# Three small edits to an attention and mixture-of-experts kernel: a padded tile, another order of the first pair's products, earlier gates for attention

## The chip, the cores and the metric

The kernel runs on one core of one Trainium2 chip. The metric is the time on the device in microseconds; the median of three runs of the kernel before is 916.73 us.

## The reference, cut to what matters

Block-causal attention (4 batches, 8 heads, 576 rows, 64 columns a head, blocks of 64 rows), and its output, laid out as 2304 rows of 512, goes through four experts whose outputs are summed with normalised weights. All is float32.

```python
scores = scale * np.matmul(q, k.transpose(0, 1, 3, 2))
scores = np.where(block_i >= block_j, scores, -1000000000.0)
attn = softmax(scores)
x = np.matmul(attn, v) 
p = domain_probs / (domain_probs.sum(-1, keepdims=True) + 1e-09)
for e in range(4):
    h = np.maximum(x @ w1[e], 0.0)      # 512 -> 1024
    out += p[:, e:e + 1] * (h @ w2[e])  # 1024 -> 512
```

## The kernel before, in words

**Precision.** A float32 product is made of three matmuls of type fp32r on split operands: each operand is a high part (a cast) and a low part (operand less high part), and high x high, high x low and low x high are summed in PSUM. Names ending in h and l are these parts (w1h, w1l, xh, xl, hh, hl). The cast is a_copy() (line 344), the subtraction tt() (line 351).

**Blocks.** The 2304 rows are five blocks (BLOCKS): block 0 is the first 64 rows of each batch (256 rows), blocks 1 to 4 the other 512 rows of batch 0 to 3. Blocks 0 to 2 go through the experts in 96 chunks (4 experts x 8 slices of 128 hidden columns, three times): chunk i is mm1(i) (line 1012: 12 matmuls that make 128 hidden columns for all rows of the block), relu(), and mm2 (line 1062: 12 matmuls that add the chunk's part to four accumulators), one chunk behind. Blocks 3 and 4 go together (both_blocks()): mm1 of both blocks for two slices of hidden columns at once is a Winograd form of Strassen's scheme, 7 products in place of 8 (product(), line 1235, 6 matmuls each), for 16 pairs j of slices; mm2_half() (line 1298) does their second layer, 48 matmuls a pair from the third pair on.

**A pair's products.** CHAIN lists the products in the order in which they are issued, each with a role 0, 1 or 2, that is, the PSUM bank that it adds to: (1,0), (2,1), (6,0), (7,2), (5,0), (4,2), (3,0). Products 1 and 2 read the x of block 3 (xh, xl), 6 reads S2, 7 S3, 5 S1, 4 A22 and 3 S4, sums and differences of the two blocks' x. Between two products of a bank a copy of the bank is taken by ScalarE (snap(), line 1255: V1 after product 1, U2 after 6, V7 after 7, U4 after 5), and the next product to that bank waits for it. SHARE says how many groups of second-layer matmuls are issued behind each product; pair 0 has only four such groups (the last chunk's mm2), which go behind products 1 and 2, and pair 1 has none.

**prepare().** When the last attention unit is through and all of attention's buffers are free, the pool attn is closed and the pool pair is laid in its place; it holds A22, S2, S3, S1 and S4 (high and low, 128 x 1024 each), four more buffers each of hh, hl and o, two more of w1h, w1l, w2h and w2l (in the trace these carry a p at the end: hhp, w1hp) and four sc. prepare() then makes, mostly on VectorE: the split of A22, s1, s3, s2, the splits of S2, S3 and S1, s4 and the split of S4, in that order.

**The pools.** The pool const holds what lives through the kernel (weights' buffers, xh, xl, hh, hl, o, XR, ident, probs_n and last probs_s). The pools attn and pair are laid behind it.

**The order of the work.** There are no hand-written queues: Flow.run() is a planner with costs for each engine. It takes one operation after the other from many generator threads by modelled start time and priority, and so fixes the order of instructions on each engine; what waits for what is then by semaphores. Attention is cut in 16 units (one batch, two heads); the first four have no gate (-1), the other twelve may start loading when the planner is at chunk gate[u], which rises in equal steps from GATES[0] to GATES[1]. A unit loads k, q and v, transposes k and q on VectorE (kT, qT), splits them (KK, HH, LL), makes the scores on TensorE (lines 520, 521), the maxima over GpSimd (mx, line 686), the exponentials on ScalarE, the sums (sa on VectorE, sb on GpSimd, line 665) and the product with v (line 732), and scales it (x of the last two blocks: tile xr, line 351).

Of the kernel before, what the change touches and what calls it, by code (L numbers as in the profile page):

```python
# [8 lines left out]
F32 = mybir.dt.float32  # L9
# [11 lines left out]
BLOCKS = [[(b, 0, MASK_BLOCK) for b in range(4)]] + [[(b, MASK_BLOCK, 576)] for b in range(4)]  # L21
# [8 lines left out]


CHAIN = [(1, 0), (2, 1), (6, 0), (7, 2), (5, 0), (4, 2), (3, 0)]
SHARE = [2, 2, 2, 3, 2, 2, 3]

GATES = (28.0, 84.0)

WARM = 9

# [171 lines left out]
def kernel(  # L210
# [14 lines left out]
    P = 128  # L225
# [37 lines left out]
    const = ctx.enter_context(tc.tile_pool(name="const", bufs=1))  # L263
# [19 lines left out]
    XR = [const.tile([P, KC, MAXW], F32, name=f"xr{g}") for g in range(2)]  # L283
    ident = const.tile([P, P], F32, name="ident")
    probs_n = const.tile([P, len(BLOCKS) * 4, E], F32, name="probs_n")
    probs_s = const.tile([P, len(BLOCKS) * 4], F32, name="probs_s")
    const.seal()
    attn = short.enter_context(tc.tile_pool(name="attn", bufs=1))
    for tag, n, shape, dt in (
# [37 lines left out]
    def op(eng, cost, fn, r=(), u=(), prio=0.0):  # L327
        p = prio if callable(prio) else (lambda: prio)
        return Op(eng, cost, fn, r, u, p)
# [18 lines left out]
    def tt(eng, dst, a, b, alu, n, r, u, prio=0.0):  # L348
        both = {"dve": 1.04 * n + 70, "pool": 2.1 * n + 365}
        engs = [(e, both[e]) for e in (eng if isinstance(eng, list) else [eng])]  # L350
        o = op(engs, 0, lambda e: ENG[e].tensor_tensor(out=dst, in0=a, in1=b, op=alu), r, u, prio)  # L351
        o.port = a.space != PSUM and b.space != PSUM
        return o
# [755 lines left out]
    def prepare():  # L1109

        yield ("until", lambda: len(raw_x) == 2 * KC and all(len(fl.free[x]) == n for x, n in counts.items()))
        base = max(b.base for x in counts for b in fl.free[x])
        short.close()
        more = ctx.enter_context(tc.tile_pool(name="pair", bufs=1, reuse_waits="tile"))

        def add(tag, n, shape, dt=F32):
            for k in range(n):
                fl.give(late_buf(more.tile(shape, dt, name=f"{tag}p{k}"), tag, base))

        def late_buf(t, tag, base):  # L1120
            b = Buf(t, tag)
            b.last = base
            return b

        names = ("A22", "S2", "S3", "S1", "S4")
        xt = {x: [late_buf(more.tile([P, 2, MAXW], F32R, name=f"{x}{y}"), None, base) for y in "hl"] for x in names}
        for y in xt.values():
            for b in y:
                b.base = base
        add("hh", 4, [P, MAXW], F32R)  # L1130
        add("hl", 4, [P, MAXW], F32R)
        add("w1h", 2, [P, DM], F32R)
        add("w1l", 2, [P, DM], F32R)
        add("w2h", 2, [P, DM], F32R)
        add("w2l", 2, [P, DM], F32R)
        add("w1r", 1, [P, KC, P])
        add("o", 4, [P, DM])
        fl.add_bufs("sc", [])
        add("sc", 4, [P, MAXW])
        n = 2 * MAXW  # L1140
        x2, x3 = [Buf(x, None) for x in XR]
        a11, a12, a21, a22 = [x[:, k:k + 2, :] for x in XR for k in (0, 2)]
        dv = [raw_x[k] for k in raw_x]

        def split(x, src, deps, u):
            hi, lo = xt[x]
            a = yield a_copy(hi.tile, src, n, deps, [hi, u], 0.5)
            l = yield tt("dve", lo.tile, src, hi.tile, SUB, n, deps + [a], [hi, lo, u], 0.5)
            xp[x] = (hi.tile, lo.tile, [a, l])
            return [a, l]  # L1150

        got = yield from split("A22", a22, dv, x3)
        s1 = yield tt("dve", a22, a21, a22, ADD, n, dv + got, [x3], 0.5)
        s3 = yield tt("dve", a21, a11, a21, SUB, n, dv + [s1], [x2, x3], 0.5)
        yield ("until", lambda: len(xready.get((PAIR, KC - 1), ())) == 2)
        old = [v for c in range(KC) for v in xready[PAIR, c]]
        s2 = yield tt("dve", a11, a22, a11, SUB, n, [s1, s3] + old, [x2, x3], 0.5)
        yield from split("S2", a11, [s2], x2)
        yield from split("S3", a21, [s3], x3)
        yield from split("S1", a22, [s1], x3)  # L1160
        s4 = yield tt("dve", a12, a12, a11, SUB, n, [s2] + old, [x2], 0.5)
        yield from split("S4", a12, [s4], x2)
        for x, r in zip((x2, x3), XR):
            for k in range(KC):
                fl.give(late_buf(r[:, k, :], "sc", x.last))
# [11 lines left out]
    def both_blocks():  # L1177

        n = MAXW
        for x, src in (("xh", "hh"), ("xl", "hl")):  # L1180
            b = yield fl.take(x, PAIR + 1)
            for k in range(KC):
                y = Buf(b.tile[:, k, :], src)
                y.last = b.base
                fl.give(y)
        yield ("until", lambda: PAIR in X and X[PAIR] is not None and "sc" in fl.free)
        xhb, xlb = X[PAIR]
        rest = [(NC - 1, t) for t in range(4)]
        for j in range(len(pairs)):
            now[0] = NC + 2 * j  # L1190
            if j > 1:
                m, t = j // 2 - 1, j % 2
                rest = [(m, t, c, k) for c in range(4) for k in range(4)]
            st, banks = {}, {}
            for (i, role), share in zip(CHAIN, SHARE):
                yield from product(j, i, role, banks, st)
                for _ in range(min(share, len(rest))):
                    x = rest.pop(0)
                    yield from (mm2(*x) if len(x) == 2 else mm2_half(*x))
            while rest:  # L1200
                x = rest.pop(0)
                yield from (mm2(*x) if len(x) == 2 else mm2_half(*x))
        now[0] = NC + 2 * len(pairs)
        for t in range(2):
            for c in range(4):
                for k in range(4):
                    yield from mm2_half(len(pairs) // 2 - 1, t, c, k)

    def product(j, i, role, banks, st):
        n = MAXW  # L1210
        yield ("until", lambda: (j, i) in wp)
        (wh, wl, va, vl), s = wp[j, i]
        if i in (1, 2):
            yield ("until", lambda: all(len(xready.get((PAIR, 2 * (i - 1) + k), ())) == 2 for k in range(2)))
            xhb, xlb = X[PAIR]
            k = slice(2 * i - 2, 2 * i)
            xh, xl, xv = xhb.tile[:, k], xlb.tile[:, k], [v for k in range(2) for v in xready[PAIR, 2 * (i - 1) + k]]
        else:
            name = {3: "S4", 4: "A22", 5: "S1", 6: "S2", 7: "S3"}[i]
            yield ("until", lambda: name in xp)  # L1220
            xh, xl, xv = xp[name]
        start = role not in banks
        if start:
            banks[role] = yield fl.take("h", None, ("att",))
        pb = banks[role]
        before = {6: "V1", 5: "U2", 3: "U4", 4: "V7"}.get(i)
        if before:
            yield ("until", lambda: before in st)
        ps = pb.tile

        def fn(_):
            for kc in range(2):
                ks = slice((2 * s + kc) * P, (2 * s + kc + 1) * P)
                for m, (w, x) in enumerate(((wh, xh), (wh, xl), (wl, xh))):
                    nc.tensor.matmul(out=ps[:, :n], lhsT=w.tile[:, ks], rhs=x[:, kc, :n], start=(start and kc == 0 and m == 0),  # L1235
                                     stop=(i in (2, 3, 4) and kc == 1 and m == 2), skip_group_check=True)

        mm = yield op("pe", 6 * (n / 2.4 + PEO), fn, [va, vl] + xv + ([st[before][1]] if before else []), [pb, wh, wl], 3.0)
        done = i in (2, 7, 4, 3)
        if done:  # L1240
            fl.give(wh, wl)
        if i in (1, 6, 5, 7):
            fl.spawn(snap(st, {1: "V1", 6: "U2", 5: "U4", 7: "V7"}[i], pb, mm))
        if i == 2:
            fl.spawn(total(j, 0, 0, st, pb, mm, "V1"))
        if i == 4:
            fl.spawn(total(j, 1, 0, st, pb, mm, "U2"))
            fl.spawn(total(j, 1, 1, st, None, None, "U4"))
        if i == 3:
            fl.spawn(relu_pair(j, 0, 1, pb, mm, True))  # L1250
# [75 lines left out]
    for ph, jobs in enumerate(PLAN):  # L1326
        for _ in range(sum(len(cs) for _, cs, _ in jobs)):
            gate.append(-1.0 if ph <= 1 else GATES[0] + (GATES[1] - GATES[0]) * (len(gate) - 4) / 11)
    u = ua = us = ju = pu = 0
# [13 lines left out]
    for c in range(KC):  # L1343
        fl.spawn(first_half(c))
    fl.spawn(prepare())
    kz = Val(2000.0, "pool")
    fl.fill = warm_up
# [44 lines left out]
```

## Time and profile before

| what | us |
| --- | --- |
| median of three runs | 916.73 |
| lowest and highest | 916.69, 922.09 |
| the profiled execution | 917.19 |
| its span, first to last instruction | 915.4 |
| TensorE busy | 900.3 |
| VectorE busy | 694.0 |
| ScalarE busy | 451.9 |
| GpSimd busy | 142.3 |

The profiled execution's time is 1.8 us more than its span. PE is TensorE, PEld its weight loads, DVE VectorE, ACT ScalarE, POOL GpSimd. L1298 is line 1298 of the kernel before. A matmul's own duration (389 ns and the like) is longer than the distance to the next one, since they are pipelined.

### The profile page before, as it was taken

Reading aid. Unit: us, or ns where it says so; the run is one execution under the profiler, and the core shown is the slowest. Engines: PE = TensorE matmul, PEld = TensorE weight load, DVE = VectorE, ACT = ScalarE, POOL = GpSimd, SP = SyncE. Lnnn points to the kernel's source line nnn. Section 1 sums busy time; section 2 is a strip of 40 time slices with the busy share of each in tenths; the row PEclk is TensorE's granted clock in tenths of the full one; section 3 lists DMA queues with packets and bytes.
Section 4 is the critical chain, followed back from the end, with each engine's and each line's share of the span. In section 5 each row is a group of like instructions: output and inputs, shape, how many; then the busy total and the mean of one; then the engine's idle time right before and its main releaser. Section 6 shows DMA issues by size and latency. Waiting matters only on the chain.

```text
span 915.4 us, 12377 instructions
## 1 busy us (share of the span) xinstructions
PE 900.3 (98%) x4301; PEld 713.8 (78%) x4302; DVE 694.0 (76%) x1296; ACT 451.9 (49%) x859; POOL 142.3 (16%) x53
## 2 busy tenths in 40 slices
PE   8999999999999999999999999799999999999998
PEld 4677788787777877877787877588888888888886
DVE  6799998797988988997988988965565655666542
ACT  3587766556546556656654543545243333333220
POOL 1101110404124134143242132000000000000000
PEclk9899999999999999999999999999999999999999
DMA  9876557463365355445435323311121212110002
GB/s 182 166 200 176 145 126 219 103 153 83 93 144 120 104 129 113 127 119 120 118 104 119 83 87 95 110 53 58 34 70 34 71 35 69 47 47 24 11 1 93
DMA packets 214655, 91.18 MB, mean 100 GB/s; under 512 B 130368, under 2 KB 195904, under 8 KB 214592
## 3 DMA queue, kind: packets, MB, share of 16 engines
q1 hardware_dynamic: 211424, 89.59, 38.4%
q10 hardware_dynamic: 3168, 0.79, 0.6%
q8 instruction: 34, 0.56, 0.3%
q14 instruction: 29, 0.24, 0.1%
HBM read 85.63 MB, written 4.72 MB: 99 GB/s over the span
## 4 chain that ended last, share of the span: by engine, by line
PE 90%; DVE 5%; SPq 2%; DMA 2%; issue 1%; ACT 0%; POOL 0%; DVEq 0%; POOLq 0%; ACTq 0%
PE h L1012 22%; PE acc L1062 22%; PE acc L1298 19%; PE h L1235 9%; PE att L1235 6%; PE att L732 4%; SPq L338 2%; PE att L520 2%; PE att L521 2%; PE att L508 1%; PE acc L732 1%; DMA S<-in_v_dram 1%; DVE o L1099 1%; PE acc L508 1%; DVE xr L351 1%
## 5 line engine op out<-in xcount | busy, mean ns | idle before, releaser
L1012 PE MATMUL h<-xl,w1h 128*128 128x512 f32 (+1 forms) x384 | 136.8, 356 | 2.1 <-DVE xl L351 2.1
L1012 PE MATMUL h<-xh,w1h 128*128 128x512 f32 (+1 forms) x384 | 137.4, 358 | 0.0
L1012 PE MATMUL h<-xh,w1l 128*128 128x512 f32 (+1 forms) x384 | 136.8, 356 | 0.0
L1062 PE MATMUL acc<-w2h,hh 128*128 128x512 f32 x320 | 126.7, 396 | 0.0
L1062 PE MATMUL acc<-w2l,hh 128*128 128x512 f32 x320 | 125.2, 391 | 0.0
L1062 PE MATMUL acc<-w2h,hl 128*128 128x512 f32 x320 | 125.1, 391 | 0.0
L665 POOL PARTITION_ALL_REDUCE sb<-sa x24 | 82.2, 3474 | 138.1 <-DVE sa L351 121.7
L344 ACT CAST w2h<-w2r 128x512 fp32r<-128x512 f32 x115 | 71.5, 622 | 55.9 <-PE acc L1062 41.7
L686 POOL PARTITION_ALL_REDUCE mx<-cm x16 | 56.0, 3499 | 277.1 <-DVE cm L351 260.6
L351 DVE TENSOR_TENSOR w2l<-w2r,w2h 128x512 fp32r<-128x512 f32 x118 | 83.3, 707 | 11.4 <-ACT w2h L344 11.2
L351 DVE TENSOR_TENSOR w1l<-w1r,w1h 128x512 fp32r<-128x512 f32 (+1 forms) x126 | 84.5, 671 | 3.9 <-ACT w1h L344 2.8
L1012 PEld LDWEIGHTS h<-xl,w1h 128*128 128x128 f32 x384 | 73.0, 190 | 13.2 <-DVE xl L351 2.5
L1012 PEld LDWEIGHTS h<-xh,w1h 128*128 128x128 f32 x384 | 72.9, 190 | 12.2 <-issue 1.2
L1012 PEld LDWEIGHTS h<-xh,w1l 128*128 128x128 f32 x384 | 73.0, 190 | 10.2
L1029 ACT ACTIVATE hh<-h 128x512 fp32r<-128x512 f32 (+1 forms) x96 | 50.5, 526 | 60.1 <-PE h L1012 59.9
L344 ACT CAST w1h<-w1r 128x512 fp32r<-128x512 f32 (+1 forms) x115 | 68.4, 595 | 14.6 <-PE att L1235 5.3
L344 ACT COPY S<-att 128x512 f32<-128x512 f32 (+2 forms) x94 | 50.5, 538 | 45.3 <-DVE att L590 34.7
L1062 PEld LDWEIGHTS acc<-w2h,hh 128*128 128x128 f32 x320 | 60.2, 188 | 12.9 <-issue 1.7
L1062 PEld LDWEIGHTS acc<-w2h,hl 128*128 128x128 f32 x320 | 60.1, 188 | 13.1
L1062 PEld LDWEIGHTS acc<-w2l,hh 128*128 128x128 f32 x320 | 60.3, 188 | 10.4
L1031 DVE SCALAR_TENSOR_TENSOR hl<-h,hh 128x512 fp32r<-128x512 f32 (+1 forms) x96 | 56.8, 592 | 10.6 <-ACT hh L1029 9.9
L351 DVE TENSOR_TENSOR S<-S,mx 128x1024 f32<-128x1024 f32 (+4 forms) x80 | 59.8, 792 | 3.0 <-POOL mx L686 3.0
(323 smaller groups left out, 1815.5 us busy)
## 6 DMA issues: line engine op xcount, KB each, us to landing
w2r<-in_moe_w_dram SPq DMA_DIRECT2D x128, 256.0 KB, 2.9
w1r<-in_moe_w_dram SPq DMA_DIRECT2D x121, 256.0 KB, 2.9
qr<-in_q_dram SPq DMA_DIRECT2D x112, 64.0 KB, 2.7
kr<-in_k_dram SPq DMA_DIRECT2D x64, 72.0 KB, 3.6
VN<-in_v_dram SPq DMA_DIRECT2D x32, 128.0 KB, 2.6
out_dram<-o SPq DMA_DIRECT2D x12, 256.0 KB, 2.1
w1rp<-in_moe_w_dram SPq DMA_DIRECT2D x7, 256.0 KB, 3.0
out_dram<-op SPq DMA_DIRECT2D x4, 256.0 KB, 2.5
```

The source lines that it names most:

```text
L338: o = op(q, 550.0, lambda e: (nc.sync if e == "sp" else nc.scalar).dma_start(out=dst, in_=src), r, u, prio)
L344: o = op(engs, 0, lambda e: nc.scalar.copy(dst, src) if e == "act" else nc.vector.tensor_copy(dst, src), r, u, prio)
L351: o = op(engs, 0, lambda e: ENG[e].tensor_tensor(out=dst, in0=a, in1=b, op=alu), r, u, prio)
L665: sums.append((yield op("pool", 150 + 6.3 * W, lambda _, h=h: nc.gpsimd.partition_all_reduce(sb.tile[:, h * W:h * W + W], sa.tile[:, h * W ...
L686: lambda _: nc.gpsimd.partition_all_reduce(mx.tile[:, :2 * W], src, P, RED.max),
L732: nc.tensor.matmul(out=x.tile[64 * g:64 * g + 64, W - w:W], lhsT=lhsT, rhs=rhs, start=(i == 0), stop=(i == len(todo) - 1))
L1012: nc.tensor.matmul(out=ps[:, :n], lhsT=s.tile[:, ks], rhs=x.tile[:, kc, :n], start=(kc == 0 and m == 0), stop=(kc == KC - 1 and m == 2),)
L1029: a = yield op("act", 0.833 * n + 55, lambda _: nc.scalar.activation(hh.tile[:, :n], ps[:, :n], AF.Relu), [mm], [pb, hh], 0.0)
L1031: l = yield op("dve", 1.04 * n + 70, lambda _: nc.vector.scalar_tensor_tensor(out=hl.tile[:, :n], in0=ps[:, :n], scalar=0.0, in1=hh.tile[: ...
L1062: nc.tensor.matmul(out=acc, lhsT=s.tile[:, ts], rhs=w.tile, start=(f == 0 and m == 0), stop=(f == FC - 1 and m == 2))
L1235: nc.tensor.matmul(out=ps[:, :n], lhsT=w.tile[:, ks], rhs=x[:, kc, :n], start=(start and kc == 0 and m == 0), stop=(i in (2, 3, 4) and kc ...
L1298: nc.tensor.matmul(out=acc, lhsT=s.tile[:, ts], rhs=w.tile, start=(c == 0 and x == 0), stop=(c == 3 and x == 2))
```

## The change

The tile probs_s gets 32 columns in place of 20 (128 bytes a partition in place of 80). Pair 0 issues its products in the order FIRST; which product gives back a pair of weight buffers is changed with it. prepare() splits S3 right after s3 is formed, ahead of s2. The last gate is chunk 82 in place of 84.

```diff
 CHAIN = [(1, 0), (2, 1), (6, 0), (7, 2), (5, 0), (4, 2), (3, 0)]
+FIRST = [(1, 0), (2, 1), (7, 2), (4, 2), (6, 0), (5, 0), (3, 0)]
 SHARE = [2, 2, 2, 3, 2, 2, 3]
-GATES = (28.0, 84.0)
+GATES = (28.0, 82.0)
...
-    probs_s = const.tile([P, len(BLOCKS) * 4], F32, name="probs_s")
+    probs_s = const.tile([P, 32], F32, name="probs_s")
...
         s3 = yield tt("dve", a21, a11, a21, SUB, n, dv + [s1], [x2, x3], 0.5)
+        yield from split("S3", a21, [s3], x3)
         yield ("until", lambda: len(xready.get((PAIR, KC - 1), ())) == 2)
         old = [v for c in range(KC) for v in xready[PAIR, c]]
         s2 = yield tt("dve", a11, a22, a11, SUB, n, [s1, s3] + old, [x2, x3], 0.5)
         yield from split("S2", a11, [s2], x2)
-        yield from split("S3", a21, [s3], x3)
         yield from split("S1", a22, [s1], x3)
...
-            for (i, role), share in zip(CHAIN, SHARE):
+            for (i, role), share in zip(CHAIN if j else FIRST, SHARE):
...
-        done = i in (2, 7, 4, 3)
+        done = i in ((2, 7, 4, 3) if j else (2, 6, 5, 3))
```

## Rows read from the trace of the kernel before

**Rows 1.** The page: busy us (share) xinstructions; chain that ended last by engine.

```profile
PE 900.3 (98%) x4301; PEld 713.8 (78%) x4302; DVE 694.0 (76%) x1296; ACT 451.9 (49%) x859; POOL 142.3 (16%) x53
...
PE 90%; DVE 5%; SPq 2%; DMA 2%; issue 1%; ACT 0%; POOL 0%; DVEq 0%; POOLq 0%; ACTq 0%
```

**Rows 2.** Windows: stretch; PE, PEld, DVE, ACT, POOL busy (x); PEclk; DMA; GB/s.

```profile
330.00:430.00 100.00, 99.92 (x474) 79.27 (x473) 89.41 (x173) 61.11 (x115) 30.80 (x9) 1.00 0.50 124
...
552.00:564.00 12.00, 12.00 (x61) 8.96 (x61) 8.86 (x15) 3.84 (x7) 6.19 (x2) 1.00 0.23 66
564.00:574.00 10.00, 10.00 (x45) 8.07 (x43) 10.00 (x15) 4.33 (x7) 0.00 (x0) 1.00 0.50 157
574.00:590.00 16.00, 11.40 (x45) 7.96 (x44) 15.93 (x25) 8.63 (x15) 0.00 (x0) 1.00 0.25 80
...
589.50:911.50 322.00, 321.88 (x1386) 260.13 (x1386) 183.29 (x317) 112.94 (x195) 0.00 (x0) 1.00 0.16 46
```

**Rows 3.** Timeline of TensorE, pairs 0 to 2: start, us, what [idle before, releaser].

```profile
573.77 0.39 PE L1062 MATMUL acc<-w2h,hl 128*128 128x512 f32 x1
574.56 0.49 PE L1235 MATMUL att<-S2h,w1h 128*128 128x512 f32 x1 [0.40 <-ACT S2h L344]
576.53 0.50 PE L1235 MATMUL att<-S2l,w1h 128*128 128x512 f32 x1 [1.48 <-DVE S2l L351]
576.86 0.40 PE L1235 MATMUL att<-S2h,w1l 128*128 128x512 f32 x1
...
586.78 0.40 PE L1235 MATMUL att<-xh,w1lp 128*128 128x512 f32 x1
589.57 0.47 PE L1235 MATMUL h<-S2h,w1h 128*128 128x512 f32 x1 [2.40 <-DVE w1h L344]
...
596.85 0.39 PE L1235 MATMUL att<-xh,w1hp 128*128 128x512 f32 x1
```

**Rows 4.** The chain that ended last, chunks of blocks 1 and 2: start, us, what.

```profile
299.43 2.72 PE h L1012 x12
302.15 2.72 PE acc L1062 x12
...
463.61 2.81 PE acc L1062 x12
```

**Rows 5.** Groups by form, line 1298: | busy us, mean ns of one | idle.

```profile
L1298 PE MATMUL acc<-w2h,hhp 128*128 128x512 f32 x84 | 33.2, 395 | 0.0
...
L1298 PE MATMUL acc<-w2hp,hh 128*128 128x512 f32 x24 | 9.5, 396 | 0.0
...
L1298 PE MATMUL acc<-w2h,hh 128*128 128x512 f32 x24 | 9.3, 389 | 0.0
...
L1298 PE MATMUL acc<-w2hp,hhp 128*128 128x512 f32 x20 | 7.8, 391 | 0.0
```

**Rows 6.** Timelines of VectorE and ScalarE: the last unit's end, prepare(), pair 1's w1h.

```profile
563.79 0.69 DVE L351 TENSOR_TENSOR xr<-xs,rc 128x512 f32<-128x512 f32 x1
...
569.75 1.22 DVE L351 TENSOR_TENSOR xr<-xr,xr 128x1024 f32<-128x1024 f32 x1
...
589.00 0.43 DVE L344 CAST w1h<-w1r 128x512 fp32r<-128x512 f32 x1
...
564.52 1.05 ACT L344 CAST A22h<-xr 128x1024 fp32r<-128x1024 f32 x1 [0.58 <-DVE xr L351]
```

**Rows 7.** Timelines of TensorE and ScalarE: a snapshot of a bank, and a cast.

```profile
569.69 0.39 PE L1235 MATMUL att<-xh,w1l 128*128 128x512 f32 x1
...
570.17 0.59 ACT L1255 COPY scp<-att 128x512 f32<-128x512 f32 x1 [2.97 <-PE att L1235]
...
573.46 1.05 ACT L344 CAST S2h<-xr 128x1024 fp32r<-128x1024 f32 x1 [2.18 <-DVE xr L351]
```

**Rows 8.** The chain that ended last, VectorE's part before 589 us: start, us, what.

```profile
581.76 1.14 DVE S4l L351
```

**Rows 9.** TensorE's waits in the whole run: us in total, times, longest.

```profile
PE att L520 <- DVE cm L351: 1.0, 1, 1.0
```

## The prediction, made before the change was run

> **What bounds the kernel now.** I read the shares of the page and the chain that ended last first: TensorE is busy for 900.3 of 915.4 us and 90% of the chain is TensorE's [rows 1]. So what an edit is worth is what it does to the spacing of matmuls and to the few places where TensorE waits. The windows by stage say where those are [rows 2]: in the stretch from 330 to 430 us TensorE is busy for 99.92 of 100 us with VectorE at 89.41; from 589.5 us on (the last two blocks) it is busy for 321.88 of 322.00 us with VectorE at 57%; only from 574 to 590 us, where the last two blocks begin, is it busy for 11.40 of 16 us, and there VectorE is busy for 15.93. The granted clock is 1.00 in all of these rows, so no part of the sum is clock. Then the timeline of TensorE through that gap [rows 3], the chain in the middle of the kernel, for what 12 matmuls cost when nothing disturbs them [rows 4], and the groups by form, for the same matmul on different tiles [rows 5].
>
> The profiled execution took 917.19 us, its span 915.4 and 1.8 around it; the median of the runs is 916.73, 0.46 less. I sum against 917.19 and take 0.4 off at the end.
>
> **Edit 1, probs_s from 80 to 128 bytes a partition.** It issues nothing; it moves addresses. Every tile of the const pool is a multiple of 64 bytes long but probs_s, the last, so the pools laid behind it (attn, then pair in its place) start off a multiple of 64, and all their tiles with them. Does an offset cost anything? The groups by form compare it: acc<-w2h,hh has both operands in const and takes 389 ns; w2hp,hhp has both in the pair pool and takes 391; w2h,hhp and w2hp,hh have one in each and take 395 and 396 [rows 5]. So what shows is not the offset but a mixture of two offsets, some 6 ns a matmul. It isn't distance: the const tiles lie up to 110 KB apart (the sum of their sizes) and are fast with each other.
>
> The price is read from spacings. Undisturbed, 12 matmuls of 512 columns take 2.72 us, 226.7 ns each, both in mm1 and mm2 [rows 4]. From 589.57 to the last matmul at about 911.3, 1386 matmuls run without a wait [rows 2, 3]: 321.7 us, 232.1 ns each. With every tile on one offset I take 226.7 for all: 1386 x 226.7 ns = 314.2 us, 7.5 us less; 0.3 of it is the ragged start after the wait, which may stay. So -7.2 us, and -7.5 to 0 as bounds: 0 if the mixture is not an affair of the offset, and a loss is excluded by the const-const group, which already has the layout that all would get. What else could bound this stage is idle enough: VectorE at 57%.
>
> In the attention stage (146 to 574 us) the tiles of attn mix with const only where a unit cuts into the stream. A group of twelve behind such a cut took 2.81 us in place of 2.72 [rows 4]. I give a cut half of that excess, 0.045 us; with 12 units and some four cuts each (three of scores, one of PV) that is 2.2 us, an estimate. Whether a cut of another length leaves the stream ragged by itself the trace doesn't show: bounds -2.2 and 0, and I take the middle, -1.0.
>
> The Trainium skill speaks against this edit. In "TensorE: Matmul & The Clock Gate", section "Step-by-step: what each phase is for", it has the weight load and the moving operand on two independent read ports that take nothing from each other, and in "SBUF — State Buffer", section "Operand start alignment", an operand only has to start on its element size, with nothing said of speed. By these pages a mixture costs nothing and the edit gives 0; the 6 ns of rows 5 say otherwise, and I go with the rows. That rule is rival B.
>
> **Edit 2, order of the first pair.** Between 573.77 (last matmul of the old block) and 596.85 (first of the third pair) stand 73 matmuls, 16.5 us at 226.7 ns; the stretch takes 23.1, so 6.5 us are lost [rows 3]: 0.56 before S2's high part and 1.7 before its low part, 2.56 before the second pair's w1h, the other 1.7 in smaller waits and restarts. Old order 6, 7, 5, 4, 3: S2 first, and S2 is the third thing that prepare() makes. New order 7, 4, 6, 5, 3: S3 and A22 first. A22 is the first thing made and s3 is formed at 569.75 [rows 6], so with S3's split right behind it (a cast of 1.05 and a subtraction of 1.2 us) S3 is done near 573, S2 near 577 and S1 and S4 1.2 to 4.6 us later, each about when its product comes up. So the 0.56 and the 1.7 go, and the smaller waits with them.
>
> But the order costs something too. Products 7 and 4 share a bank, 6, 5 and 3 another, and the snapshot of the bank must be read by ScalarE before the next product adds to it. In the old order another product always stood between. In the new one 7-4, 6-5 and 5-3 are neighbours, and the four left-over mm2 groups are used up after products 1 and 2. One bare snapshot: the last matmul of product 1 starts at 569.69 and lasts 0.39, the copy starts 0.09 later at 570.17 and lasts 0.59, and a cast that ends (573.46 + 1.05) releases TensorE 0.05 later, at 574.56 [rows 3, 7]: 1.12 us from start to start in place of 0.23, so 0.9, and 0.1 for the next matmul, which comes after 0.33 us (576.53 to 576.86). Three of them: +3.0 us. Bounds: 2.7, and 6.1 if ScalarE is each time at a 1.05 us cast first.
>
> **Edit 3, gates up to chunk 82.** The gates rise by 4.91 chunks in place of 5.09; rounded up, the last unit opens two chunks earlier and the eleven before it up to one. No work is added: TensorE is full there, so what moves forward only changes places. Its use is at the end: the last unit's product is at 563.79 and prepare() starts at 564.52 [rows 6]. A chunk is 5.4 us without attention, 6.6 with it; the last unit also waits for the one before, so I take prepare() 6 to 11 us earlier. What hides in this is VectorE: it is full from 574.68 to the w1h cast at 589.00 that TensorE waited 2.4 us for, and 6.3 us of that are prepare()'s (S2l, S3l, S1l, s4 and S4l, each at some 1.14 like S4l [rows 8], and S4h at about half). If prepare() is over before 574, that cast comes at about 583; TensorE asks for it at 586.5 (573.8 + 43 x 0.227 + 3.0). So the 2.56 goes, with 3.5 us to spare. Without the shift it stays: bounds -2.6 and 0, I take -2.6. In the earlier part VectorE has 1.1 of 10 us left, and 3.1 of 12 from 552 to 564 [rows 2]; denser by 3.7% it still fits.
>
> Late next at the transition are then only the three snapshots: 6.5 - 3.0 = -3.5 us (bounds -3.8 to 0).
>
> **Sum.** 917.2 - 7.2 - 1.0 - 3.5 - 0.4 = **905.1 us**. About 1% (9.2 us) is what a measurement of this kernel can tell from no change; it lies at 907.6.
>
> **Rivals.**
> - B, the two-port rule holds, the mixture isn't the offset: edit 1 gives 0 and the rest 3.5. 917.2 - 3.5 - 0.4 = 913.3 us. For it: no row compares tiles that differ in offset alone. Against it: the pair-pair group is as fast as const-const. 0.08.
> - D, the transition gives nothing: snapshots stand in ScalarE's queue behind casts (+6.1) or VectorE's backlog keeps the 2.56. 917.2 - 7.2 - 0.6 - 0.4 = 909.0 us. For it: VectorE is full from 564 to 590 [rows 2], and three bare waits are certain by the order. Against: two chunks of shift. 0.20.
> - C, the other side: VectorE becomes the bound of the denser attention stage. At present one score matmul in the whole run waited for VectorE's cm, 1.0 us [rows 9]. Two such waits a unit, 24 x 1.0, bring 905.1 + 24 = 929 us; it decides from 12 waits on, where the gain is used up. For it: 89% of VectorE in rows 2. Against: 56/54 of that is 93%. 0.04.
> - All of edit 1's and edit 3's bounds at their best (cuts clean, transition at 2.5 us): 903 us, part of the forecast.
>
> **Chances.** Forecast 0.68 with its own range of 902.5 to 908; D 0.20 at 907.5 to 911; B 0.08 at 911 to 914; C 0.04. The range 902.5 to 911 leaves out B, C and a little below, 0.15. Faster by over 1%: most of the forecast and a little of D, 0.70; within 1%: 0.27; slower 0.03.
>
> **What would show it.** Edit 1: w2h,hhp and w2hp,hh at 389 to 391 ns like the others, and the 1386 matmuls of the last stage in about 314.5 us. If they stay at 395, B. Edit 2: three gaps of about 0.9 us behind products 7, 6 and 5, ended by ScalarE's copies, and none ended by S2, S3 or S4. Edit 3: prepare()'s A22 cast at or before 558 us, and no wait of TensorE for w1h at the second pair; a wait of 2 us or more there is D. Waits of score matmuls for cm in many units would be C.

## The result and the profile after

The changed kernel takes 909.83 us (median of six runs, 909.16 to 910.62) against 917.92 for the kernel before in the same comparison: a ratio of 0.9899, 95% interval 0.9882 to 0.9916. It is faster by about 1%, 8 us. I had forecast 905.1 with a range of 902.5 to 911.0, so the direction and the range held, and a third of the gain that I had summed did not come. The time lies in the band of rival D (907.5 to 911), not in the forecast's own (902.5 to 908). The profiled execution took 909.63 us, its span went from 915.4 to 907.6.

The first line of the changed kernel's page and the busy times of its engines, to be held against [rows 1]:

```profile
span 907.6 us, 12364 instructions
...
PE 896.4 (99%) x4302; PEld 714.6 (79%) x4302; DVE 692.5 (76%) x1298; ACT 451.3 (50%) x857; POOL 140.5 (15%) x53
```

Two timeline rows cut the span in three parts whose gains can be compared: the last matmul of the old blocks (mm2 of chunk 95), and the first matmul of the third pair. The stretch between the two is called the transition. Before they stand at 573.77 and 596.85 [rows 3]; after, with the rows between them where TensorE waited, the timeline of TensorE is (lines are one further on: L1063 is L1062 of before, L1236 is L1235, L1299 is L1298):

```profile
570.19 0.39 PE L1063 MATMUL acc<-w2h,hlp 128*128 128x512 f32 x1
570.41 0.39 PE L1236 MATMUL h<-S3h,w1h 128*128 128x512 f32 x1
...
571.58 0.40 PE L1236 MATMUL h<-S3h,w1l 128*128 128x512 f32 x1
572.65 0.50 PE L1236 MATMUL h<-A22h,w1hp 128*128 128x512 f32 x1 [0.68 <-ACT scp L1256]
...
575.31 0.39 PE L1236 MATMUL att<-S2h,w1l 128*128 128x512 f32 x1
576.38 0.50 PE L1236 MATMUL att<-S1h,w1hp 128*128 128x512 f32 x1 [0.68 <-ACT scp L1256]
...
577.64 0.40 PE L1236 MATMUL att<-S1h,w1lp 128*128 128x512 f32 x1
579.31 0.50 PE L1236 MATMUL att<-S4h,w1h 128*128 128x512 f32 x1 [1.27 <-ACT scp L1256]
...
583.38 0.39 PE L1236 MATMUL att<-xh,w1lp 128*128 128x512 f32 x1
583.61 0.39 PE L1236 MATMUL h<-S2h,w1h 128*128 128x512 f32 x1
...
590.61 0.40 PE L1236 MATMUL att<-xh,w1hp 128*128 128x512 f32 x1
```

The reader is to see here that no product waits for S2, S3 or S4 any more, that pair 1's S2 product at 583.61 follows the matmul at 583.38 without a wait for w1h, and that three waits stand in their place, each ended by a snapshot (scp): the price of edit 2 as I had read it.

| part | before, us | after, us | gain | foretold |
| --- | --- | --- | --- | --- |
| up to the last matmul of the old blocks | 573.77 | 570.19 | 3.6 | 1.0 |
| from there to the third pair (the transition) | 23.08 | 20.42 | 2.7 | 3.5 |
| from the third pair to the end of the span | 318.6 | 317.0 | 1.5 | 7.2 (all of the last stage) |

(The third pair's first matmul stands at 590.61 in the changed kernel; 907.6 less that is 317.0.) So what failed is the last stage, and the first part gave more than I had any term for. Of its 3.6 us, 0.9 lie before chunk 32 (146.81 before, 145.91 after), whose start differs from run to run as said below. The groups by form of the changed kernel, to be held against [rows 5]:

```profile
L1299 PE MATMUL acc<-w2h,hhp 128*128 128x512 f32 x80 | 31.5, 394 | 0.0
...
L1299 PE MATMUL acc<-w2h,hh 128*128 128x512 f32 x28 | 11.0, 391 | 0.0
...
L1299 PE MATMUL acc<-w2hp,hhp 128*128 128x512 f32 x24 | 9.4, 391 | 0.0
...
L1299 PE MATMUL acc<-w2hp,hh 128*128 128x512 f32 x20 | 7.9, 394 | 0.0
```

A mixture of a const and a pair tile still costs, 394 ns against 391, though both pools now start on a multiple of 64 bytes. Either the mixture has nothing to do with the offset (rival B), or 64 bytes are not the unit.

### The profile page after: what moved, and what is told of

It is laid out like the page before. It is cut to its first block, busy times and chain, and to the rows that moved or that the text cites. A ratio compares the mean times of both kernels' runs of the same rounds, so it can differ in the third digit from the quotient of the medians.

```text
span 907.6 us, 12364 instructions
## 1 busy us (share of the span) xinstructions
PE 896.4 (99%) x4302; PEld 714.6 (79%) x4302; DVE 692.5 (76%) x1298; ACT 451.3 (50%) x857; POOL 140.5 (15%) x53
## 4 chain that ended last, share of the span: by engine, by line
PE 92%; DVE 3%; DMA 2%; SPq 1%; ACT 0%; issue 0%; DVEq 0%; ACTq 0%
PE h L1013 23%; PE acc L1063 23%; PE acc L1299 20%; PE h L1236 9%; PE att L1236 7%; PE att L733 4%; PE att L521 2%; PE att L522 2%; SPq L339 1%; PE acc L733 1%; PE att L509 1%; DMA S<-in_v_dram 1%; DVE xr L352 1%; PE acc L509 1%; DMA probs_n<-in_moe_domain_probs_dram 0%; DMA cm<-in_q_dram 0%
## 5 line engine op out<-in xcount | busy, mean ns | idle before, releaser
L1063 PE MATMUL acc<-w2h,hh 128*128 128x512 f32 x316 | 125.2, 396 | 0.0
L1063 PE MATMUL acc<-w2l,hh 128*128 128x512 f32 x316 | 123.5, 391 | 0.0
L1063 PE MATMUL acc<-w2h,hl 128*128 128x512 f32 x316 | 123.3, 390 | 0.0
L352 DVE TENSOR_TENSOR w1l<-w1r,w1h 128x512 fp32r<-128x512 f32 (+1 forms) x124 | 86.7, 699 | 1.6 <-ACT w1h L345 0.6
L352 DVE TENSOR_TENSOR w2l<-w2r,w2h 128x512 fp32r<-128x512 f32 x117 | 79.7, 682 | 4.9 <-ACT w2h L345 4.6
L345 ACT CAST w1h<-w1r 128x512 fp32r<-128x512 f32 (+1 forms) x111 | 66.1, 596 | 17.5 <-DMA w1r<-in_moe_w_dram 9.6
L1063 PEld LDWEIGHTS acc<-w2h,hl 128*128 128x128 f32 x316 | 59.3, 188 | 13.1
L1063 PEld LDWEIGHTS acc<-w2h,hh 128*128 128x128 f32 x316 | 59.5, 188 | 12.8 <-issue 1.7
L1063 PEld LDWEIGHTS acc<-w2l,hh 128*128 128x128 f32 x316 | 59.5, 188 | 10.4
```

The source lines that it names most:

```text
L345: o = op(engs, 0, lambda e: nc.scalar.copy(dst, src) if e == "act" else nc.vector.tensor_copy(dst, src), r, u, prio)
L1063: nc.tensor.matmul(out=acc, lhsT=s.tile[:, ts], rhs=w.tile, start=(f == 0 and m == 0), stop=(f == FC - 1 and m == 2))
```

## The experiments

**The offset.** I took two theories. S: the offset between the two operands' tiles counts, in a unit longer than 64 bytes. What pointed to it: the matmuls' tiles in const lie multiples of 2048 bytes apart, and the slices of 128 columns that are loaded as weights multiples of 512, and all of these are fast with each other. Adding up the sizes, pair stood 416 bytes past a multiple of 512 from them before and 448 after; 64 bytes more (probs_s of 48 columns) make it a multiple of 512. (The sizes before add up to 400 past such a multiple; 416 takes it that a pool starts on a multiple of 32 bytes, which no run shows. The other distances don't hang on that.) P: what counts is that the tiles belong to two pools far from each other.

The first run is edit 1 alone, the next the changed kernel without it, and then three other sizes of probs_s in the changed kernel.

```diff
 # e1_pad32_alone, against the kernel before
-    probs_s = const.tile([P, len(BLOCKS) * 4], F32, name="probs_s")
+    probs_s = const.tile([P, 32], F32, name="probs_s")
```

> The kernel before with edit 1 alone (probs_s of 128 bytes), the same order of instructions. Theory S (what counts is the offset between the two operands' tiles in a unit longer than 64 bytes; after the change the pools stand 448 bytes apart modulo 512 in place of 416): the mixture still costs, the last two blocks' 1386 matmuls take some 320 us in place of 321.7 and the whole 1 to 2.5 us less than before. Rival U (64 bytes are the unit and something else spoils the last stage of the changed kernel, its order say): the 1386 take about 314.5 us and the whole 7 us less.

```diff
 # e2_no_pad, against the changed kernel
-    probs_s = const.tile([P, 32], F32, name="probs_s")
+    probs_s = const.tile([P, len(BLOCKS) * 4], F32, name="probs_s")
```

> The changed kernel with probs_s back at 80 bytes, the same order of instructions: edits 2 and 3 alone. If the three parts add up, it gives what edit 1 doesn't: the transition 2.6 us shorter than before, the stage of attention some 2.5 to 3.5 us shorter, the last stage as before, 911.5 us in all. If edit 1 gave the shorter attention stage as well, 914.

```diff
 # e3_pad48, against the changed kernel; e7_pad80 and e8_pad112 likewise with 80 and 112
-    probs_s = const.tile([P, 32], F32, name="probs_s")
+    probs_s = const.tile([P, 48], F32, name="probs_s")
```

> The changed kernel with probs_s of 192 bytes: the pools behind it then stand a multiple of 512 bytes from the tiles of const, as the tiles and 128-column slices of const stand to each other. Theory S: a mixture costs nothing any more, w2h,hhp and w2hp,hh fall from 395 to 390 ns, the last stage loses some 5 us (1386 matmuls at 227 ns) and the attention stage 1 to 2, so 903 us. Rival P (what counts is that the tiles are of two pools, far from each other, and no offset): nothing moves, 909.8 us.

> The changed kernel with probs_s of 320 bytes: pair stands 128 bytes past a multiple of 512 from the tiles of const. It looks for the unit. If 128 bytes are the unit, all matmuls of the last stage come 226.7 ns apart as with 192 bytes; if it is 256 or 512, a mixture costs again, some 3 to 7 ns, and the stage from the third pair on takes 311 to 314 us in place of 307.

> The changed kernel with probs_s of 448 bytes: pair stands 256 bytes past a multiple of 512 from the tiles of const. If the unit is 256 bytes or a part of it, 226.7 ns for all and 307 us from the third pair on; if it is 512, a mixture costs and the stage takes 311 to 314 us.

And, to have the price in the kernel for which it was predicted, the kernel before with 48 columns and no other edit:

```diff
 # e11_before_pad48, against the kernel before
-    probs_s = const.tile([P, len(BLOCKS) * 4], F32, name="probs_s")
+    probs_s = const.tile([P, 48], F32, name="probs_s")
```

> The kernel before with probs_s of 192 bytes and nothing else: the price of the mixture alone, in the kernel on which it was predicted. Theory S: the stage from the third pair on takes 307.1 us in place of 314.2, the attention stage some 1.5 us less, the transition unchanged at 23 us: 8.5 us less than before, a ratio of 0.9907. If the effects of the offset and of the order are not independent, the sum with edits 2 and 3 alone (5.5 us) will miss the 13.3 us of the changed kernel with 192 bytes.

Measured (the ratio is to the kernel before in the same comparison; the fourth column is each profiled span less the start of its third pair, 4.3 us more in the changed kernel than the time up to the last matmul, by which most of the expectations go; e7 and e8 are one run each):

| run | probs_s bytes | past a multiple of 256 | third pair to end, us | median us | ratio (95%) |
| --- | --- | --- | --- | --- | --- |
| before | 80 | 160 | 318.6 | 917.92 | |
| e2_no_pad | 80 | 160 | 318.6 | 912.26 | 0.9941 (0.9926 to 0.9956) |
| e1_pad32_alone | 128 | 192 | 317.0 | 915.80 | 0.9981 (0.9967 to 0.9995) |
| after | 128 | 192 | 317.0 | 909.83 | 0.9899 (0.9882 to 0.9916) |
| e7_pad80 | 320 | 128 | 317.0 | 909.30 | one run |
| e3_pad48 | 192 | 0 | 311.5 | 904.52 | 0.9853 (0.9837 to 0.9869) |
| e8_pad112 | 448 | 0 | 311.5 | 902.75 | one run |
| e11_before_pad48 | 192 | 0 | 311.5 | 909.43 | 0.9920 (0.9889 to 0.9950) |

The groups by form of the run with 192 bytes:

```profile
L1299 PE MATMUL acc<-w2h,hhp 128*128 128x512 f32 x80 | 31.1, 389 | 0.0
...
L1299 PE MATMUL acc<-w2h,hh 128*128 128x512 f32 x28 | 10.9, 389 | 0.0
...
L1299 PE MATMUL acc<-w2hp,hhp 128*128 128x512 f32 x24 | 9.3, 389 | 0.0
...
L1299 PE MATMUL acc<-w2hp,hh 128*128 128x512 f32 x20 | 7.8, 389 | 0.0
```

All four combinations take 389 ns, and the window from the third pair on shows the same work in the shorter time; first the changed kernel, then the run with 192 bytes (columns as in [rows 2]):

```profile
590.60:903.60 313.00, 313.00 (x1357) 254.34 (x1355) 176.73 (x304) 108.27 (x186) 0.00 (x0) 1.00 0.15 44
```

```profile
592.00:899.40 307.40, 307.40 (x1357) 254.40 (x1355) 176.37 (x305) 108.46 (x187) 0.00 (x0) 1.00 0.15 45
```

From the third pair to the last matmul there are 1356 (the windows count one more at their edge): 313.0 and 307.4 us are 230.8 and 226.7 ns each. Theory P falls: nothing but 64 bytes of padding lies between the two runs. Of the five distances tried, 0 and 256 past a multiple of 512 cost nothing, and 128, 416 and 448 do; so the unit is 256 bytes as far as these show. At 128 and at 192 past it the price is the same, 5.5 us in this stage, at 160 it is 7.1.

Is it the place of pair by itself that costs, or its distance from const? The timeline of the kernel before answers that. From its third pair on, the matmuls with one operand in each pool (756) are followed by the next one after 233.6 ns on average, those with both operands in one pool (599) after 229.8. Of the latter, those with six neighbours of the same pool on either side are undisturbed, in const (92 of them, 226.9) and in pair (27 of them, 227.1). So the place of pair costs nothing by itself, and the matmuls of one pool are slowed only near others. With 192 bytes both means are 226.7.

The rule of the Trainium skill, "TensorE: Matmul & The Clock Gate", section "Step-by-step: what each phase is for", that a weight load takes nothing from the running matmul since both have a read port of their own, would have the padding change nothing, and the runs differ by 5.5 us in this stage. That it is a weight load and the running matmul's moving operand that disturb each other fits a price that falls on neighbours too, but no run shows it by itself. The Trainium skill's "SBUF — State Buffer", section "Operand start alignment", says that its rule is about legality and not speed, and no run here is at odds with that.

The run e11 gives the price in the kernel before: 7.1 us in the last stage (318.6 to 311.5), 1.7 in the stage of attention (from chunk 32's first matmul to the last mm2, 426.96 to 425.27), and 8.5 us of the median, as expected. Its transition did not stay at 23.1, it takes 24.35: the waits are those of before, but behind the one for w1h the granted clock fell to 0.50 (1.2 GHz), and the nine matmuls behind that wait took 3.76 us in place of 2.38. Its 8.5 us and the 5.5 of e2 add up to 14.0, against 13.3 for both together (e3), no difference at this noise.

e1 and e2 also part the first two thirds of the time. Edit 1 alone shortens the stage of attention by 0.6 us, 426.96 to 426.35; edits 2 and 3 without it by 2.3, to 424.64. I had edit 1 at 1.0 there and edit 3 at nothing. Of e1's 0.6 us, 0.4 are a shorter wait of a score matmul for cm (0.6 us in place of 1.0 [rows 9]); in e2 that wait is gone, and in the changed kernel. What the other 1.3 us of e2 are I didn't take apart. The first matmul of chunk 32 itself stands anywhere between 145.0 and 148.8 us in the twelve profiled runs, whatever the edit, so a run's time moves by some microseconds that none of the edits accounts for, and stages are compared here by their own length.

**The transition.** Are the gates or the order what shortens it?

```diff
 # e4_gates84, against the changed kernel
-GATES = (28.0, 82.0)
+GATES = (28.0, 84.0)
```

> The changed kernel with the gates up to chunk 84 again: edits 1 and 2 alone. If edit 3 is what lets prepare() finish in time, the three snapshots' waits (3.1 us) stay and the second pair's wait for w1h of some 2.5 us is back, and the attention stage is as long as before: 914 to 916 us. If the order alone gives the gain at the transition and the gates nothing, 910.

```diff
 # e5_chain_order, against the changed kernel
-            for (i, role), share in zip(CHAIN if j else FIRST, SHARE):
+            for (i, role), share in zip(CHAIN, SHARE):
...
-        done = i in ((2, 7, 4, 3) if j else (2, 6, 5, 3))
+        done = i in (2, 7, 4, 3)
```

> The changed kernel with pair 0's products in the old order (6, 7, 5, 4, 3), S3 still split ahead of s2. By the reading of the changed kernel's trace (three bare snapshots cost 3.1 us, while S3l is done at 566.1, S2l at 570.3, S1l at 574.0 and S4l at 577.4) the old order would wait about 0.2 us for S2, 0.9 for S1 and 0.5 for S4 and for no snapshot: the transition takes 18.3 us in place of 20.4 and the whole 2 us less than the changed kernel, 907.7. If S2 and the weights come later than that for want of VectorE, as the order was meant to avoid, the transition takes 21 us or more and the whole 910 or more.

e4_gates84 took 914.19 us (0.9964, 0.9945 to 0.9984), its transition 22.7 us; e5_chain_order 913.79 us (0.9942, 0.9918 to 0.9965), its transition 22.8. Before it was 23.1, with both edits 20.4. So as measured neither does it alone: each gives 0.3 or 0.4 us, both together 2.7. (S3's earlier split is in all of these but the kernel before, and was not tried alone.) Where the waits went is in the waits of TensorE of the two runs, first the gates up to 84, then the old order:

```profile
PE att L1236 <- ACT scp L1256: 1.9, 2, 1.2
...
PE att L1236 <- DVE S2l L352: 1.0, 1, 1.0
...
PE h L1236 <- ACT scp L1256: 0.7, 1, 0.7
```

```profile
PE h L1236 <- DVE w1h L345: 2.4, 1, 2.4
...
PE att L1236 <- DVE S4l L352: 0.5, 1, 0.5
...
PE att L1236 <- DVE S1l L352: 0.4, 1, 0.4
```

With the late gates the new order pays for its three snapshots and still waits for S2 (and 0.4 us for S3); pair 1's wait for w1h, which I expected back, is not there. With the old order there is no wait for a snapshot, and S1 and S4 cost 0.9 us by these rows (1.4 computed); but the 2.4 us for w1h are back, the other branch of what I expected, so prepare() being early does not by itself bring that cast in time. The wait for w1h goes with the order, under either gates. The rows of that cast, in the changed kernel, with the gates up to 84, and with the old order:

```profile
579.42 0.62 ACT L345 CAST w1h<-w1rp 128x512 fp32r<-128x512 f32 x1 [0.17 <-DVE w1rp L352]
```

```profile
583.89 0.62 ACT L345 CAST w1h<-w1r 128x512 fp32r<-128x512 f32 x1 [0.53 <-DVE w1r L352]
```

```profile
585.55 0.43 DVE L345 CAST w1h<-w1rp 128x512 fp32r<-128x512 f32 x1
```

In both kernels with the new order the cast is over before TensorE asks for it (583.61 in the changed kernel, about 590.5 with the late gates). With the old order it moved forward from 589.00 [rows 6] to 585.55, no further than TensorE itself, whose last matmul before the wait moved from 586.78 [rows 3] to 583.34: 3.4 us each, and so the wait stayed. Why the planner places the cast so late with the old order stays open.

What costs on top in the run with the old order is the clock, in the windows behind that wait:

```profile
584.00:586.00 2.00, 0.00 (x0) 0.00 (x0) 1.95 (x4) 0.78 (x2) 0.00 (x0) 1.00 0.54 138
...
587.00:588.00 1.00, 1.00 (x3) 0.81 (x4) 1.00 (x3) 0.32 (x1) 0.00 (x0) 0.50 0.01 4
588.00:590.00 2.00, 2.00 (x6) 1.51 (x6) 1.97 (x5) 1.19 (x3) 0.00 (x0) 0.50 0.49 138
```

TensorE stood still from 583.7 to 586.1, and from about 587 to 590 its granted clock was 0.50, 1.2 GHz; one matmul came 0.59 and six 0.43 us after the one before in place of 0.23, 1.6 us in all. In the kernel before a wait as long, 2.40 us, was followed by a clock of 1.00. So some 21.2 of the 22.8 us are the order's, still 0.8 over the changed kernel's 20.4. Without the clock, then, the earlier gates give 1.9 us with the old order, the new order 0.4 with the old gates, and both 2.7. By this the gates do most of it, as far as the 1.6 us can be taken off.

**Fewer bare snapshots.** Two of the three waits can be had for nothing: in the order 7, 6, 4, 5, 3 product 6 stands between 7 and 4, and 4 between 6 and 5. Tried with 192 bytes:

```diff
 # e6_pad48_order, against the changed kernel
-    probs_s = const.tile([P, 32], F32, name="probs_s")
+    probs_s = const.tile([P, 48], F32, name="probs_s")
...
-FIRST = [(1, 0), (2, 1), (7, 2), (4, 2), (6, 0), (5, 0), (3, 0)]
+FIRST = [(1, 0), (2, 1), (7, 2), (6, 0), (4, 2), (5, 0), (3, 0)]
```

> The kernel with probs_s of 192 bytes, with pair 0 in the order 7, 6, 4, 5, 3: V7's snapshot goes beside product 6 and U2's beside product 4, only U4's stays bare. If the snapshots are what the transition waits for, two gaps of 0.85 us go; the last wait, for S4 and U4 together, grows to some 2 us, since S4l is done no earlier: the transition 18.6 us in place of 20.15, and the whole 903 us. If S4's lateness takes it all back, 904.5.

903.64 us (0.9845, 0.9824 to 0.9867): not measurably better than 192 bytes alone, and its transition takes 21.7 us, more than the 20.15 with 192 bytes alone and far from the 18.6 expected. Two snapshots' waits went, and a wait for the next weights came, as this row of TensorE's waits shows, with VectorE's rows for the split that it waited for and the operation ahead of it:

```profile
PE h L1236 <- DVE w1l L352: 1.0, 1, 1.0
```

```profile
583.29 0.69 DVE L352 TENSOR_TENSOR xr<-att,xr 128x512 f32<-128x512 f32 x1 [1.05 <-PE att L1236]
583.90 0.68 DVE L352 TENSOR_TENSOR w1l<-w1rp,w1h 128x512 fp32r<-128x512 f32 x1
```

On VectorE three w2 splits, which nobody asks for before the third pair, stood ahead of that w1 split, and right ahead of it an operation for which VectorE itself waited 1.05 us for TensorE. The planner gives them the same priority, so I raised that of w1 for pairs 1 and 2:

```diff
 # e9_w1_first, against e6_pad48_order
     def w_prio(i, which):
+        if which == 1 and NC + 2 <= i < NC + 6: return lambda: 0.7
         i -= 4 * (i >= NC) * (which == 1)
```

> The kernel with probs_s of 192 bytes and the order 7, 6, 4, 5, 3, and the planner's priority of the splits of pairs 1 and 2's w1 raised above that of w2. In the run with that order the two bare snapshots of V7 and U2 were gone, and a wait for w1l of 1.0 us at pair 1 was new, because three w2 splits stood ahead of it on VectorE. If VectorE's order is all that the transition still hangs on, the w1 wait goes and the transition takes 18.5 to 19.5 us in place of 21.7 and of 20.15: 902 us or a little less. If S4l's lateness (it stands behind the same splits) takes the gain, the transition stays above 20 us and the time at 903.6 to 904.5.

901.85 us, a ratio of 0.9836 (0.9810 to 0.9862), the lowest median of all, though its interval overlaps those of e3 and e6; the transition takes 19.2 us. In the list of TensorE's waits no weight is left, and of the transition these two:

```profile
PE att L1236 <- ACT scp L1256: 1.3, 1, 1.3
...
PE att L1236 <- DVE S4l L352: 0.4, 1, 0.4
```

## Why the prediction was right, and where it was not

That the range held is in part luck. The last stage gave 5.7 us less than foretold and the transition 0.8 less, while the time before the transition fell by 2.6 us more than its term; without these 2.6 the changed kernel would have stood at 912.4, outside the range.

**Edit 1, the last stage: the price was right and its condition wrong.** I gave the mixture 7.2 us in the last stage; 192 bytes of probs_s take 7.1 us from the third pair on in the kernel before (318.6 to 311.5). The step that failed is "with every tile on one offset I take 226.7 for all": a start on a multiple of 64 bytes is not one offset for this purpose. The pools went from 160 to 192 bytes past a multiple of 256, and that is worth 1.5 us. I took the unit from the diff, not from a row, and said "a loss is excluded by the const-const group, which already has the layout that all would get": that group has it, tiles that lie 256 bytes' multiples apart, but the changed pools don't. The zero end of my bounds was for another reason (rival B, no affair of the offset), which the runs refute.

**Edit 1, the attention stage.** Foretold -1.0, measured -0.6 (e1_pad32_alone), mostly the shorter wait for cm and not the price of a cut. What the offset is worth there without a wait is 1.3 us, 424.64 to 423.33 from e2 to e3, and the edit as made gives 0.4 of it (424.64 to 424.28).

**Edit 2.** Three bare snapshots at 1.0 each: 572.65 less 571.58 is 1.07, and 576.38 less 575.31 the same, 0.84 each over the undisturbed 0.23, and a tenth for the restart: right. The third is 1.67 from start to start, because ScalarE was at another operation first, as in my upper bound:

```profile
578.15 0.63 ACT L1279 ACTIVATE hhp<-scp 128x512 fp32r<-128x512 f32 x1 [1.52 <-DVE scp L352]
578.69 0.57 ACT L1256 COPY scp<-att 128x512 f32<-128x512 f32 x1
```

Together that is 3.4 us for the 3.0 foretold. The transition fell 0.8 short in all; the other 0.4 fits the mixture, which still slows its 73 matmuls. The waits for S2 and S4 went.

**Edit 3.** The A22 cast starts at 557.57 in place of 564.52, seven microseconds earlier, within my 6 to 11; but TensorE itself reached the pairs 3.6 us earlier, which I left out, so prepare() gained 3.4 us on it, not 7. S4l ends at 577.5, not before 574. The wait for w1h is gone in the changed kernel all the same, but not by the shift alone, as I had it: with the old order and the same gates it stands at 2.4 us. The step that failed is "if prepare() is over before 574, that cast comes at about 583": with the old order the cast only moved as far as TensorE did. So I had the two edits the wrong way round. The 2.6 us for w1h, which I credited to edit 3, came with edit 2's order: there is no such wait with it under either gates. The 2.3 us of waits for S2, which I credited to edit 2, went with edit 3's gates: none is left with the old order (e5), and 1.2 are with the new order and the late gates (e4: S2h 0.2, S2l 1.0). The sum of the two came out near, its shares did not. That edit 3 would shorten the stage of attention I did not foresee: by 1.8 us, 426.08 with the gates up to 84 (e4) to 424.28 in the changed kernel.

**The rivals.** B is refuted by the runs with 192 and 448 bytes. D named the weak place of the transition, and the time came near its own (909.0) by another way, since the transition did give 2.7 us. (The 0.6 in D's sum has no row behind it; with the 1.0 of the attention stage it would be 908.6.) C did not occur: no score matmul waits for cm in the changed kernel, and VectorE is busy for 86.52 us from 330 to 430.

## What to carry to other kernels

Where a matmul's two operands come from tiles laid out at different times, compare the groups by form for the same shape on different tiles: a few nanoseconds between them can be an address effect, and over the 1356 matmuls here they were 7 us. Then try the distance between the pools: here a multiple of 256 bytes cost nothing, and other multiples of 64 did. And before a wait is removed, look at what the full engine behind it does next: here the order of the products, the time of their operands and the order of the weight splits on VectorE had to be right together.

## What the runs showed of the hardware that was not expected

Where all operands of a stream of 128x512 fp32r matmuls, with a weight load each, lay a multiple of 256 bytes apart, a matmul took 389 ns and the next came 226.7 ns behind it. Where part of the stream had its two operands 128, 416 or 448 bytes past a multiple of 512 apart, these matmuls took 394 to 396 ns; in the kernel before the next came 233.6 ns behind them on average. Those near them with both operands in one pool were slowed as well (389 to 391 ns, 229.8). One offset for all tiles in SBUF is not needed for it: const and pair lay 256 bytes past a multiple of 512 apart with 448 bytes of probs_s, and the stage took the same 311.5 us.

A wait of TensorE of 2.4 us was followed by some three microseconds at a granted clock of 0.50 in two profiled executions (2.40 us in e5_chain_order, 2.44 in e11_before_pad48) and by a clock of 1.00 in two others (2.40 in the kernel before, and the same wait in e1_pad32_alone). These are e11's wait and a window behind it, and a window behind the wait of the kernel before:

```profile
586.12 0.49 PE L1235 MATMUL h<-S2h,w1h 128*128 128x512 f32 x1 [2.44 <-DVE w1h L344]
```

```profile
587.00:588.00 1.00, 1.00 (x4) 0.81 (x4) 1.00 (x3) 0.33 (x1) 0.00 (x0) 0.50 0.01 2
```

```profile
590.00:592.00 2.00, 2.00 (x10) 1.48 (x9) 2.00 (x5) 1.20 (x3) 0.00 (x0) 1.00 0.08 29
```

What decides between the two the runs don't show.
